# Attention with mixed heads and two dense layers: v fetched later, scores one round later, and a first tile that loads from two queues and writes to three pairs of banks

## Chip, cores and metric

One core of one Trainium2 chip. The metric is the device time of one execution in microseconds (us), median of several runs. Engines are named as in the profile: PE (TensorE matmul), PEld (its weight loads), DVE (VectorE), ACT (ScalarE), POOL (GpSimd), SP (SyncE, which here issues the transfers).

## What is computed

Attention over 4 batches, 12 heads, 448 positions, head size 64, in which the heads are mixed before and after the softmax, and then two dense layers over 448 x 768 a batch. The change touches the attention part alone.

```python
scores = scale * np.matmul(q, k.transpose(0, 1, 3, 2))
scores = np.einsum('bhij,hg->bgij', scores, w_pre)
scores = scores - np.max(scores, axis=-1, keepdims=True)
attn = np.exp(scores)
attn = attn / (np.sum(attn, axis=-1, keepdims=True) + 1e-09)
attn = np.einsum('bhij,hg->bgij', attn, w_post)
return np.matmul(attn, v).astype(np.float32)
```

After it come a gated layer (`_moe_ref`: tanh gelu, a norm, a product over the positions, an output product with the residual) and a second one with sines and cosines (`_moe2_ref`).

## The kernel before

**Tiles and rounds.** Each batch's 448 query rows are cut into tiles of 120, 120, 120 and 88 rows (TILES, line 23): 16 tiles in all, numbered 0 to 15 through the batches; `first` and `last` give a tile's first and last round. A round handles two groups of ten query rows with all their 12 heads. A tile of 120 rows has six rounds, one of 88 rows has five, the last of which holds a single group of eight rows: 92 rounds. Tiles 4, 8 and 12 are the first of batches 1 to 3.

**What a round does** (the loop `for r in range(-LR, NR + 7)`, lines 329 to 358). The order on every engine is the order in which the program issues, written out by hand. Round r issues: `relayout(r + 4)`, two transfers on SP from the tile's score buffer `s` into two of six buffers `blk`; the list `early` (loads and stores); `postmix(r)` on PE; the weights of r + 1 on DVE and POOL (`recip2`, `weigh`); `at_copy(r)` on ACT and DVE; the lists `front` and `mid`; `premix(r + 2)` on PE, `rowmax` on DVE, `expo` on ACT, `recip` on POOL; then the lists `work` and `late`. Each list is filled with `put(list, round, function, arguments)`.

**Scores.** `scores(b, t, c)` makes two of a tile's 12 heads; six units c = 0 to 5 make the tile's `s`. A unit's matmuls (line 130) write two PSUM banks, and ACT copies both with one instruction into `s` (line 137). The pool psA holds one pair of banks; in the first two tiles every other unit takes two banks of psC instead, and DVE copies them (line 134). There are two `s` buffers: tile T's first copy overwrites the buffer of tile T - 2 and waits until that tile's last relayout has landed. `units(T)` (line 277) spreads a tile's six units over the rounds from `first[T - 1] - 4` to `first[T] - 5`. The first unit of a round goes to `front`, ahead of premix; if a round has a second one, it goes to `work`, behind premix. So far a round holds one unit, save the first round of tiles 4, 8 and 12, whose units have five rounds.

**Loads.** All transfers are issued by SP in program order: q of a tile three rounds ahead of its units, k of a batch in the rounds of the units of the tile before the batch's first, v in four parts from round f - 14 on, three rounds apart, f being the batch's first round (line 294); for batch 0 in rounds 1 to 4. v has two buffers, which the batches take in turn. It is read by `attn_v` (lines 242 and 246), whose first unit for a tile stands one round behind the tile's last round. `relayout` (line 148) also waits until the `blk` that it overwrites has been read by `premix` three rounds before.

**The start.** Eight matmuls on zeros warm PE up; SP issues q of tile 0, the six k and small constants; then the six units of tile 0 run, and the loop begins at round -4.

**Beside the rounds** ACT, DVE and POOL decode the weights `w_in` of the first dense layer (lines 484 to 511), in rounds 8 to 85. The dense part follows from about 346 us.

Of the kernel before, what the change touches and what calls it, by code (L numbers as in the profile page):

```python
# [6 lines left out]
F32 = mybir.dt.float32  # L7
# [4 lines left out]
AF = mybir.ActivationFunctionType  # L12
# [4 lines left out]
B, H, S, D = 4, 12, 448, 64  # L17
# [5 lines left out]
TILES = [(t0, min(TI, S - t0)) for t0 in range(0, S, TI)]  # L23
HALF = [n // IB * SQ for t0, n in TILES]
SKIP = [64 - h for h in HALF]
QCOLS = [p + NP * n for p, (t0, n) in zip(SKIP, TILES)]
AW = [-(-n // IB) * SQ for t0, n in TILES]
AM, AX3 = 2 * 3 * H, 2 * 3 * H + H
LR, LQ = 4, 2
# [5 lines left out]
def attention(tc, nc, io, xT, B, extra, tail):  # L35
# [9 lines left out]
    tiles = [(b, t) for b in range(B) for t in range(len(TILES))]  # L45
    nt = len(tiles)
    first, last = {}, {}
# [4 lines left out]
    with ExitStack() as es:  # L52
        early_es = ExitStack()

        def pool(name, bufs, **kw):
            return es.enter_context(tc.tile_pool(name=name, bufs=bufs, reuse_waits="tile", **kw))

        def pool_r(name, bufs, **kw):
            return early_es.enter_context(tc.tile_pool(name=name, bufs=bufs, side="right", reuse_waits="tile", **kw))
# [6 lines left out]
        psA = pool_r("psA", 1, space=PSUM)  # L66
# [7 lines left out]
        psB = pool("psB", 2, space=PSUM)  # L74
        psC = pool("psC", 2, space=PSUM)
# [4 lines left out]
        ps = psC.tile([128, 512], F32, tag="psC", name="warm_ps")  # L80
# [3 lines left out]
        kpre = cp.tile([128, 2, 64], F32, name="kpre")  # L84
# [6 lines left out]

        kt, qt = {}, {}

        def load_k(b, c):
            kt[b, c] = k_p.tile([128, S], F32, tag="k", name="k")
            nc.sync.dma_start(out=kt[b, c], in_=io["kvT"][b, 128 * c:128 * c + 128, 0])

        def load_q(b, t):
            n, o = QCOLS[t], sum(QCOLS[:t])
            qt[b, t] = q_p.tile([128, max(QCOLS)], F32, tag="q", name="q")  # L100
            nc.sync.dma_start(out=qt[b, t][:, :n], in_=io["qT"][b, :, o:o + n])

        vt = [p.tile([128, 4, NP, 128], F32, tag="v", name="v") for p in (vr_p, v_p)]

# [6 lines left out]
        st = {}  # L111

        def scores(b, t, c):

            n = TILES[t][1]
            if c == 0:
                st[b, t] = s_p.tile([128, H, S], F32, tag="s", name="s")
            q, k, o = qt[b, t], kt[b, c], c * n
            m = 64 + n - HALF[t]
            apart = b == 0 and t < 2 and c % 2  # L120
            if apart:
                ps = [psC.tile([128, 512], F32, tag="psC", name="psA") for _ in range(2)]
            else:
                pair = psA.tile([128, 2, 512], F32, tag="psA", name="psA")
                ps = [pair[:, e] for e in range(2)]
            for h in range(2):
                r = slice(64 * h, (64, m)[h])
                for e in range(2):
                    p = slice(64 * e, 64 * e + 64)
                    nc.tensor.matmul(ps[e][r, :S], q[p, o + r.start:o + r.stop], k[p], start=True, stop=True)  # L130
            out = st[b, t][:m, 2 * c:2 * c + 2]
            if apart:
                for e in range(2):
                    nc.vector.tensor_scalar(out=out[:, e], in0=ps[e][:m, :S], scalar1=0.125, scalar2=None,  # L134
                                            op0=ALU.mult)
            else:
                nc.scalar.activation(out=out, in_=pair[:m, :, :S], func=AF.Copy, scale=0.125)  # L137
# [4 lines left out]
        def relayout(r):  # L142
            b, t, k, step, m, n = pairs[r]
            sblk[r] = [blks[2 * (r % 3) + e] for e in range(m)]
            p = 64 - n // 2 * H
            for e, blk in enumerate(sblk[r]):
                o = SKIP[t] + k + e
                nc.sync.dma_start(out=blk[p:p + n * H], in_=st[b, t][o:o + step * (n - 1) + 1:step])

        def premix(r):  # L150
            ps = mix[r] = [psB.tile([128, 512], F32, tag="psB", name="psB") for _ in sblk[r]]
# [120 lines left out]
        early, front, mid, work, late = {}, {}, {}, {}, {}  # L272

        def put(d, r, fn, *a):
            d.setdefault(r, []).append((fn, a))

        def units(T):
            lo, hi = first[tiles[T - 1]] - LR, first[tiles[T]] - LR - 1
            return [lo + (c * (hi - lo + 1)) // NP for c in range(NP)]

        for T in range(1, nt):
            b, t = tiles[T]
            u = units(T)
            for c in range(NP):
                put(front if u[c] not in u[:c] else work, u[c], scores, b, t, c)
            if T > 1:
                put(early, u[0] - QO, load_q, b, t)
            if t == 0:
                for c, r in enumerate(units(T - 1)):
                    put(early, r, load_k, b, c)  # L290
        for b in range(B):
            f = first[b, 0]
            for j in range(4):
                put(early, f - 14 + 3 * j if b else 1 + j, load_v, b, j)
        for T in range(nt):
            b, t = tiles[T]
            for c in range(NP):
                if T == nt - 1:
                    r = last[b, t] + 1 + c // 3
                else:  # L300
                    r = last[b, t] + (min(2 + c, 6) if T == 0 else min(1 + c, 5 if t == 2 else 6))
# [5 lines left out]
        for j, fn in enumerate(extra):  # L307
            r = JR0 + (NR - JR0 - JR1) * j // len(extra)
# [8 lines left out]
            put(early, r + 4, fn[5], dec)  # L317


        load_q(0, 0)  # L320
        for c in range(NP):
            load_k(0, c)
            if c == 1:
                nc.sync.dma_start(out=kpre, in_=io["kpre"].rearrange("p (o c) -> p o c", o=2))
        load_q(0, 1)
        for c in range(NP):
            scores(0, 0, c)
# [785 lines left out]
def build(tc, nc, io, out):  # L1113
    with tc.manual_schedule(), ExitStack() as top:
        dram = top.enter_context(tc.tile_pool(name="scratch", bufs=1, space=bass.MemoryType.DRAM))
        xT = dram.tile([DM, B * S], F32, name="xT")
        x2T = dram.tile([DM, B * S], F32, name="x2T")
        d = Dense(tc, nc, io, xT, x2T, out)
        d.scratch(dram)
        right, left1, left2 = ExitStack(), ExitStack(), ExitStack()  # L1120
        tail, win_es, last_u, end = moe1(d, left1, right)
        th_es = moe2(d, left2, win_es, last_u, left1)
        for i in range(4):
            tail.setdefault(-2 + 2 * i, []).append(d.step)
        slots = top.enter_context(ExitStack())
        d.open_slots(slots)
        jobs = []
        for half, ks in ((1, range(KD)), (0, range(KE))):
            for k in ks:
                jobs += d.decode_tiles(io["w_in"], slice(128 * k, 128 * k + 128), HF * half, HF * half + HF,  # L1130
                                       lambda k=k, half=half: d.pieces(k, half))
        attention(tc, nc, io, xT, B, jobs, tail)
        while d.at < len(d.units):
            d.step()
        th_es.close()
        right.close()
        slots.close()
        left2.close()
# [69 lines left out]
```

## Time and profile before

| | us |
|---|---|
| median of 3 runs | 867.61 (865.63 to 867.61) |
| the profiled execution | 866.24 |
| its span in the trace | 864.5 |
| PE busy | 842.7 (97%) |
| DVE busy | 592.1 (68%) |
| ACT busy | 493.6 (57%) |
| POOL busy | 204.6 (24%) |

The page gives a share of busy time for the whole span, and a chain of work that ended last, followed back from the last instruction. The busy time of PE is that of matmuls that overlap, so a busy PE is not one at its peak. What a round costs is read from the timeline: the distances from the start of a block of matmuls to the start of the next. In timelines, equal neighbours are merged into one line with their count; a bracket at the end tells how long the engine stood idle before, and what ended that.

### The profile page before, as it was taken

How to read it: one execution, taken by the hardware profiler on the slowest of the kernel's cores; microseconds unless marked ns; L12 is line 12 of the kernel's file. 1: busy time of each engine (PE TensorE's matmuls, PEld its weight loads, DVE VectorE, ACT ScalarE, POOL GpSimd, SP SyncE). 2: the span in 40 equal slices, each digit the busy share in tenths (PEclk: the TensorE clock that was granted, in tenths of full speed). 3: DMA queues.
4: the chain of work that ended last, by engine and by line, in shares of the span. 5: the costliest groups of instructions: out<-in, count | busy, mean ns of one | idle time of the engine just before them, and what ended most of it. 6: DMA issues, size and time to landing. Idle time of an engine off the chain costs nothing.

```text
span 864.5 us, 27167 instructions
## 1 busy us (share of the span) xinstructions
PE 842.7 (97%) x10984; PEld 664.9 (77%) x10984; DVE 592.1 (68%) x1364; ACT 493.6 (57%) x1106; POOL 204.6 (24%) x404
## 2 busy tenths in 40 slices
PE   7999999899989999999999999999999999999998
PEld 2465666466656666798988989898999999999997
DVE  5566676467666776879999998779784378338231
ACT  3688788579877886584845767247443155025010
POOL 0222223122222222000000000038228047306321
PEclk9999999899999999999999999999999999999999
DMA  5667657565776546551757867997611221300301
GB/s 195 212 223 227 196 180 229 179 201 172 249 202 209 177 158 167 153 159 50 247 180 240 270 196 230 351 299 230 214 38 45 83 54 31 118 19 1 118 11 64
DMA packets 108877, 142.16 MB, mean 164 GB/s; under 512 B 25680, under 2 KB 94800, under 8 KB 108752
## 3 DMA queue, kind: packets, MB, share of 16 engines
q1 hardware_dynamic: 108752, 140.42, 51.4%
q8 instruction: 87, 1.43, 0.7%
q14 instruction: 38, 0.31, 0.1%
HBM read 74.26 MB, written 27.59 MB: 118 GB/s over the span
## 4 chain that ended last, share of the span: by engine, by line
PE 91%; issue 3%; DMA 2%; DVE 2%; ACT 1%; POOL 0%; ACTq 0%; POOLq 0%; DVEq 0%; SPq 0%
PE ps L442 55%; PE psB L156 8%; PE psD L242 8%; PE psA L130 8%; PE psC L201 7%; PE psD L246 3%; DMA blk<-s 2%; PE psC L206 1%; PE ps L960 1%; DMA x<-x2T 1%; ACT s L137 0%; ACT e L170 0%; DVE s L134 0%; POOL x2s L438 0%; POOL z L438 0%
## 5 line engine op out<-in xcount | busy, mean ns | idle before, releaser
L170 ACT ACTIVATE e<-psB,nmx 128x448 f32<-128x448 f32 x180 | 112.3, 629 | 49.0 <-DVE nmx L162 47.3
L162 DVE TENSOR_REDUCE nmx<-psB 128x1 f32<-128x448 f32 x180 | 104.1, 619 | 27.9 <-PE psB L156 26.1
L442 PE MATMUL ps<-wtok,z 128*128 128x448 f32 x504 | 104.8, 368 | 0.0
L130 PE MATMUL psA<-k,q 64*64 64x448 f32 (+2 forms) x768 | 93.7, 547 | 10.1 <-ACT s L137 8.0
L242 PEld LDWEIGHTS psD<-at,v 128*64 128x64 f32 x1152 | 56.5, 137 | 60.6 <-issue 39.9
L442 PEld LDWEIGHTS ps<-wtok,z 128*128 128x128 f32 x504 | 94.6, 188 | 9.5
L156 PE MATMUL psB<-blk,kpre 64*64 64x448 f32 x720 | 97.9, 541 | 1.9 <-DMA blk<-s 1.1
L442 PE MATMUL ps<-wth,x2s 128*128 128x384 f32 x504 | 94.2, 342 | 2.4 <-POOL x2s L438 1.8
L137 ACT ACTIVATE s<-psA 124x896 f32<-124x896 f32 (+1 forms) x90 | 82.7, 919 | 24.0 <-PE psA L130 12.2
L438 POOL TENSOR_TENSOR x2s<-x,x2s 128x384 fp32r<-128x384 f32 x28 | 28.8, 1047 | 278.2 <-DMA xres<-xT 201.8
L442 PEld LDWEIGHTS ps<-wth,x2s 128*128 128x128 f32 x504 | 88.1, 188 | 4.1 <-POOL x2s L438 2.8
L442 PE MATMUL ps<-u,wch 128*128 128x448 f32 x432 | 89.9, 368 | 0.0
L442 PEld LDWEIGHTS ps<-u,wch 128*128 128x128 f32 x432 | 81.0, 188 | 8.1
L201 PE MATMUL psC<-wr,e 64*64 64x60 f32 x4320 | 83.4, 220 | 1.7 <-issue 1.1
L201 PEld LDWEIGHTS psC<-wr,e 64*64 64x64 f32 x4320 | 74.1, 136 | 8.6 <-POOL wr L188 5.3
L242 PE MATMUL psD<-at,v 128*64 128x120 f32 (+1 forms) x1152 | 77.3, 269 | 0.0
L438 POOL TENSOR_TENSOR z<-zz,z 128x384 fp32r<-128x384 f32 x56 | 63.8, 1159 | 56.4 <-ACT z L435 56.3
L435 ACT ACTIVATE u<-xres 128x448 fp32r<-128x448 f32 x24 | 13.8, 577 | 98.1 <-DVE xres L1021 98.1
L156 PEld LDWEIGHTS psB<-blk,kpre 64*64 64x64 f32 x720 | 36.7, 132 | 42.5 <-issue 19.3
L176 POOL TENSOR_SCALAR rc<-sum 128x2 f32<-128x2 f32 (+1 forms) x92 | 17.9, 195 | 210.5 <-ACT e L170 210.5
L188 POOL TENSOR_SCALAR wr<-wts,rc 128x60 f32<-128x60 f32 x180 | 54.1, 314 | 48.1 <-DVE rc L181 36.5
L442 PE MATMUL ps<-slot,x 128*128 128x512 f32 x252 | 60.1, 396 | 0.0
(111 smaller groups left out, 1437.6 us busy)
## 6 DMA issues: line engine op xcount, KB each, us to landing
blk<-s SPq DMA_DIRECT2D x176, 210.0 KB
draw<-in_w_in SPq DMA_DIRECT2D x24, 256.0 KB
k<-in_kvT SPq DMA_DIRECT2D x24, 224.0 KB
xraw<-xT SPq DMA_DIRECT2D x24, 224.0 KB
xres<-xT SPq DMA_DIRECT2D x24, 224.0 KB
x2T<-xres SPq DMA_DIRECT2D x24, 224.0 KB
xres<-x2T SPq DMA_DIRECT2D x24, 224.0 KB
out<-uu SPq DMA_DIRECT2D x24, 224.0 KB
```

The source lines that it names most:

```text
L130: nc.tensor.matmul(ps[e][r, :S], q[p, o + r.start:o + r.stop], k[p], start=True, stop=True)
L137: nc.scalar.activation(out=out, in_=pair[:m, :, :S], func=AF.Copy, scale=0.125)
L156: nc.tensor.matmul(ps[e][c:c + 64, :S], kpre[k, e], blk[k], start=True, stop=True)
L162: nc.vector.tensor_reduce(out=nmx[r][:, e:e + 1], in_=ps[:, :S], axis=AX.X, op=ALU.max, negate=True)
L170: nc.scalar.activation(out=x, in_=ps[:, :S], func=AF.Exp, bias=m[:, e:e + 1], accum_out=sm[:, e:e + 1])
L176: nc.gpsimd.tensor_scalar(out=rc[:, :m], in0=sm[:, :m], scalar1=1e-9, scalar2=1.0, op0=ALU.add, op1=ALU.mult)
L188: nc.gpsimd.tensor_scalar(out=w, in0=wts, scalar1=rc[:, e:e + 1], scalar2=0.0, op0=ALU.mult, op1=ALU.add)
L201: nc.tensor.matmul(pc[r][h][c:c + 64, o:o + H], x[p, 128 * jc + c:128 * jc + c + 64], w[p], start=(e == 0 and jc == 0), stop=(not two and ...
L242: nc.tensor.matmul(ps[p], v[:, jc, p], main[:, H * jc + 2 * c + i], start=(o == 0 and jc == 0), stop=False)
L246: nc.tensor.matmul(px[p] if e else ps[p, 0], v[q, 3, p], rest[q, 2 * c + i], start=(o == 0 and e == 1), stop=(o > TI))
L438: eng.tensor_tensor(out=out, in0=in_, in1=hi.bitcast(F32), op=ALU.subtract)
L442: self.nc.tensor.matmul(ps, l, r, start=(i == 0), stop=(i == len(terms) - 1))
```

## The change

1. `load_v` for batches 1 to 3 goes from rounds f - 14, - 11, - 8, - 5 to f - 3, - 1, + 1, + 3.
2. `units(T)` begins one round later for every tile but tile 1, and ends in the same round. `load_q`, which stands three rounds ahead of the first unit, and the k loads, which use `units`, move with it.
3. In tile 0 the units take psA, psC and psB in turn (c % 3). Of a unit in psB, ACT copies one bank and DVE the other.
4. At the start, q of tile 0 is loaded in two parts, the first with what units 0 and 1 need; k 0, 2, 4 and kpre are issued by ACT, k 1, 3, 5 by SP.
5. In rounds 0 to 2 the second of a relayout's two transfers is issued by ACT.

```diff
--- before.py
+++ after.py
@@ -91,14 +91,15 @@
 
         kt, qt = {}, {}
 
-        def load_k(b, c):
+        def load_k(b, c, eng=nc.sync):
             kt[b, c] = k_p.tile([128, S], F32, tag="k", name="k")
-            nc.sync.dma_start(out=kt[b, c], in_=io["kvT"][b, 128 * c:128 * c + 128, 0])
-
-        def load_q(b, t):
-            n, o = QCOLS[t], sum(QCOLS[:t])
+            eng.dma_start(out=kt[b, c], in_=io["kvT"][b, 128 * c:128 * c + 128, 0])
+
+        def load_q(b, t, parts=None):
+            o = sum(QCOLS[:t])
             qt[b, t] = q_p.tile([128, max(QCOLS)], F32, tag="q", name="q")
-            nc.sync.dma_start(out=qt[b, t][:, :n], in_=io["qT"][b, :, o:o + n])
+            for m, n in parts or ((0, QCOLS[t]),):
+                nc.sync.dma_start(out=qt[b, t][:, m:n], in_=io["qT"][b, :, o + m:o + n])
 
         vt = [p.tile([128, 4, NP, 128], F32, tag="v", name="v") for p in (vr_p, v_p)]
 
@@ -117,9 +118,10 @@
                 st[b, t] = s_p.tile([128, H, S], F32, tag="s", name="s")
             q, k, o = qt[b, t], kt[b, c], c * n
             m = 64 + n - HALF[t]
-            apart = b == 0 and t < 2 and c % 2
+            apart = b == 0 and (c % 3 if t == 0 else t == 1 and c % 2)
             if apart:
-                ps = [psC.tile([128, 512], F32, tag="psC", name="psA") for _ in range(2)]
+                p, tag = (psC, "psC") if apart == 1 else (psB, "psB")
+                ps = [p.tile([128, 512], F32, tag=tag, name="psA") for _ in range(2)]
             else:
                 pair = psA.tile([128, 2, 512], F32, tag="psA", name="psA")
                 ps = [pair[:, e] for e in range(2)]
@@ -131,6 +133,9 @@
             out = st[b, t][:m, 2 * c:2 * c + 2]
             if apart:
                 for e in range(2):
+                    if apart == 2 and not e:
+                        nc.scalar.activation(out=out[:, e], in_=ps[e][:m, :S], func=AF.Copy, scale=0.125)
+                        continue
                     nc.vector.tensor_scalar(out=out[:, e], in0=ps[e][:m, :S], scalar1=0.125, scalar2=None,
                                             op0=ALU.mult)
             else:
@@ -145,7 +150,8 @@
             p = 64 - n // 2 * H
             for e, blk in enumerate(sblk[r]):
                 o = SKIP[t] + k + e
-                nc.sync.dma_start(out=blk[p:p + n * H], in_=st[b, t][o:o + step * (n - 1) + 1:step])
+                eng = nc.scalar if e and r < 3 else nc.sync
+                eng.dma_start(out=blk[p:p + n * H], in_=st[b, t][o:o + step * (n - 1) + 1:step])
 
         def premix(r):
             ps = mix[r] = [psB.tile([128, 512], F32, tag="psB", name="psB") for _ in sblk[r]]
@@ -275,7 +281,7 @@
             d.setdefault(r, []).append((fn, a))
 
         def units(T):
-            lo, hi = first[tiles[T - 1]] - LR, first[tiles[T]] - LR - 1
+            lo, hi = first[tiles[T - 1]] - LR + (T > 1), first[tiles[T]] - LR - 1
             return [lo + (c * (hi - lo + 1)) // NP for c in range(NP)]
 
         for T in range(1, nt):
@@ -291,7 +297,7 @@
         for b in range(B):
             f = first[b, 0]
             for j in range(4):
-                put(early, f - 14 + 3 * j if b else 1 + j, load_v, b, j)
+                put(early, f - 3 + 2 * j if b else 1 + j, load_v, b, j)
         for T in range(nt):
             b, t = tiles[T]
             for c in range(NP):
@@ -317,11 +323,12 @@
             put(early, r + 4, fn[5], dec)
 
 
-        load_q(0, 0)
+        n = 2 * TILES[0][1] + SKIP[0]
+        load_q(0, 0, ((0, n), (n, QCOLS[0])))
         for c in range(NP):
-            load_k(0, c)
-            if c == 1:
-                nc.sync.dma_start(out=kpre, in_=io["kpre"].rearrange("p (o c) -> p o c", o=2))
+            load_k(0, c, (nc.scalar, nc.sync)[c % 2])
+            if c == 0:
+                nc.scalar.dma_start(out=kpre, in_=io["kpre"].rearrange("p (o c) -> p o c", o=2))
         load_q(0, 1)
         for c in range(NP):
             scores(0, 0, c)
```

## Rows read from the trace of the kernel before

**Rows 1.** The page's chain of work that ended last, shares of the span.
```profile
PE 91%; issue 3%; DMA 2%; DVE 2%; ACT 1%; POOL 0%; ACTq 0%; POOLq 0%; DVEq 0%; SPq 0%
```

**Rows 2.** Timeline of PE, ordinary round: start us, us, engine, line, count, [idle].
```profile
58.52 0.84 PE L242 MATMUL psD<-at,v 128*64 128x120 f32 x12
...
59.45 0.88 PE L201 MATMUL psC<-wr,e 64*64 64x60 f32 x48
...
60.27 0.93 PE L130 MATMUL psA<-k,q 64*64 64x448 f32 x8
61.02 0.93 PE L156 MATMUL psB<-blk,kpre 64*64 64x448 f32 x8
61.88 0.84 PE L242 MATMUL psD<-at,v 128*64 128x120 f32 x12
```

**Rows 3.** Timeline of PE, two rounds of the last tile without scores.
```profile
320.60 1.49 PE L156 MATMUL psB<-blk,kpre 64*64 64x448 f32 x8
...
323.76 1.47 PE L156 MATMUL psB<-blk,kpre 64*64 64x448 f32 x8
```

**Rows 4.** Timeline of PE, rounds beside the weighted sum of an 88-row tile.
```profile
287.55 0.93 PE L156 MATMUL psB<-blk,kpre 64*64 64x448 f32 x8
288.41 0.69 PE L242 MATMUL psD<-at,v 128*64 128x90 f32 x12
...
290.76 0.93 PE L156 MATMUL psB<-blk,kpre 64*64 64x448 f32 x8
```

**Rows 5.** Timeline of PE, second scores of tiles 4, 8, 12.
```profile
74.97 0.98 PE L130 MATMUL psA<-k,q 64*64 64x448 f32 x8 [1.29 <-ACT s L137]
75.88 0.84 PE L242 MATMUL psD<-at,v 128*64 128x120 f32 x12
...
78.39 0.93 PE L156 MATMUL psB<-blk,kpre 64*64 64x448 f32 x8
...
159.01 1.76 PE L130 MATMUL psA<-k,q 64*64 64x448 f32 x8 [4.25 <-ACT s L137]
...
164.97 0.54 PE L156 MATMUL psB<-blk,kpre 64*64 64x448 f32 x4
...
243.35 0.98 PE L130 MATMUL psA<-k,q 64*64 64x448 f32 x8 [2.17 <-ACT s L137]
```

**Rows 6.** Timelines of SP (issues) and of ACT ahead of tile 8's first copy.
```profile
147.53 0.63 SPq L108 DMA_DIRECT2D v<-in_vN  x1
148.26 1.05 SPq L476 DMA_DIRECT2D draw<-in_w_in  x1
149.41 1.69 SPq L148 DMA_DIRECT2D blk<-s  x2
...
158.04 0.92 ACT L137 ACTIVATE s<-psA 124x896 f32<-124x896 f32 x1 [4.11 <-DMA blk<-s]
```

**Rows 7.** Busy time by stretch; last: granted PE clock, DMA share, GB/s.
```profile
160.00:162.00 2.00, 2.00 (x20) 1.09 (x12) 0.00 (x0) 1.75 (x5) 0.19 (x1) 0.50 0.85 247
```

**Rows 8.** Timeline of ACT in the ordinary round: copy of scores, second exponential.
```profile
61.27 0.92 ACT L137 ACTIVATE s<-psA 112x896 f32<-112x896 f32 x1
...
63.37 0.62 ACT L170 ACTIVATE e<-psB,nmx 128x448 f32<-128x448 f32 x1
63.89 0.20 ACT L170 ACTIVATION_READ_ACCUMULATOR e<-psB,nmx 128x1 f32 x1
```

**Rows 9.** Timeline of all engines, from warm-up to first premix.
```profile
1.20 3.34 PE L82 MATMUL warm_ps<-warm 128*128 128x512 f16 x8 [1.20 <-DVE warm L79]
...
10.95 1.15 DVE L134 TENSOR_SCALAR s<-psA 124x448 f32<-124x448 f32 x2 [1.07 <-PE psA L130]
...
12.18 6.84 SPq L148 DMA_DIRECT2D blk<-s  x8
...
15.11 1.50 PE L156 MATMUL psB<-blk,kpre 64*64 64x448 f32 x5 [1.14 <-DMA blk<-s]
16.01 0.14 PEld L156 LDWEIGHTS psB<-blk,kpre 64*64 64x64 f32 x3 [0.71 <-DMA blk<-s]
```

**Rows 10.** Busy time by stretch at the start, columns as in group 7.
```profile
2.00:8.00 6.00, 5.32 (x35) 1.85 (x37) 2.97 (x7) 0.95 (x3) 0.00 (x0) 1.00 0.97 338
13.50:20.00 6.50, 4.64 (x32) 1.07 (x24) 2.64 (x7) 2.26 (x5) 0.59 (x3) 1.00 0.63 239
```

## Prediction, written before the changed kernel was built or run

> **What bounds the kernel now.** I read the chain that ended last first [rows 1]: 91% of the span is TensorE, and only small pieces are something else ("DMA blk<-s" 2%, "issue" 3%). So a change gains only where TensorE stands still, and it loses wherever it makes TensorE stand still. The change touches the attention part (to about 346 us of 864.5); what follows is TensorE from end to end and moves with it.
>
> Next the timeline of TensorE in an ordinary round [rows 2]. I call the blocks V (weighted sum, line 242 and 246), M (postmix, 201 and 206), S (scores, 130) and P (premix, 156). They stand back to back: V 0.93 us from start to start (58.52 to 59.45), M 0.82, S 0.75, P 0.86: a round is 3.36 us, and TensorE sets it. In the last tile's rounds, which hold no S, a round is 3.16 us (320.60 to 323.76) although TensorE has only 2.6 us of work: there P is drawn out to 1.48 us, because the loop premix, row maximum, exponential, premix (two banks) sets the pace [rows 3]. A round without S is thus only 3.36 - 3.16 = 0.20 us shorter. That number carries the forecast. While V runs on an 88-row tile's 90 columns the round is 3.21 us [rows 4].
>
> Last, where TensorE stands still. Three rounds (tiles 4, 8 and 12, the first tile of batches 1 to 3) hold two S units. There ACT's copy of the first unit waits for the relayout transfers of the tile two back, whose buffer it overwrites, and TensorE waits for the copy, since the one pair of banks psA is busy: 1.29, 4.25 and 2.17 us [rows 5]. The second shows the cause best: the last relayout was issued from 149.41 on, not two microseconds behind a part of v, and ACT stood 4.11 us until 158.04 [rows 6].
>
> **Part 1: scores one round later.** units() starts a tile's six units one round later and ends them in the same round. Six units that had six rounds now have five: the first round holds none, the second holds two. For tiles 4, 8 and 12 (five rounds) it becomes four rounds, two of them double, where there was one.
>
> What it removes: the waits. Of each gap, 0.29 us would be there in any double round (P's row ends 0.93 after its start, at 61.95; the second S could start at 62.24, below). 1.29 + 4.25 + 2.17 - 3 x 0.29 = 6.84 us. After the 4.25 us, TensorE ran at 0.50 of its clock, that is at 1.2 instead of 2.4 GHz [rows 7]: from the late S to the next P took 5.96 us (159.01 to 164.97), where tile 4 took 3.42 (74.97 to 78.39), 2.54 us more [rows 5]. Together 9.4 us. One round more is 3.2 us and part 2 lightens the queue, so I take all of it away.
>
> What it adds: the price of a unit that is second in its round. In the ordinary round, ACT copies the first unit from 61.27 to 62.19 [rows 8] and TensorE follows 0.05 us later (74.92 to 74.97 in [rows 5]), at 62.24; without a second unit V would have started at 61.88 [rows 2]. That is 0.36 us of waiting. The unit itself takes 0.91 us (74.97 to 75.88). Then the next round's S needs psA again: its copy stands on ACT behind both exponentials, whose last reading ends at 63.89 + 0.20 = 64.09 [rows 8], so it ends at 65.01 and S may start at 65.06; TensorE would be there at 61.88 + 0.36 + 0.91 + 0.93 + 0.82 = 64.90. Another 0.15 us. A second unit costs 1.42 us, the empty round gives back 0.20: 1.22 us for a tile. Where V is short (tiles 6, 10, 14) the empty round gives back 3.21 - 3.16 = 0.05 and the wait for psA is 0.15 longer: 1.42 + 0.15 - 0.05 = 1.52 us. Tiles 2 to 15 are affected; 4, 8 and 12 get one more double and one empty round, the same 1.22. Tile 2 has no V beside its units; I give it 1.22 too, with 0.6 and 2.3 as ends. Sum: 11 x 1.22 + 3 x 1.52 = 18.0 us. The three doubles that exist today will have the 0.15 us wait again once ACT is no longer late, 0.45, so the stalls give back 8.9 net.
>
> From below, a second unit would cost only its matmuls less the empty round (0.75 - 0.20 = 0.55 a tile, 7.7 us in all) if ACT's copies were hidden; from above 1.6 a tile plus 2.3 (some 23 us), where w_in's decoding puts two more ACT instructions ahead of the second copy.
>
> **Part 2: v ten rounds later.** The same twenty transfers. v is first read six rounds after its batch's first tile begins, and the last quarter is issued three rounds after that begin: three rounds, 10 us, cover a landing that at the worst place today took about 7.6 us (150.3 to 158.0 in [rows 6]). The new place has no k loads beside it. I cost it at nothing; what is queued behind v on SP is the next relayout, needed two rounds later. Uncovered, each late v would cost what it is late. Its gain is already in part 1's 9.4.
>
> **Part 3: the first tile.** Today TensorE's six units alternate between psA and psC and end with DVE's copies at 10.95 + 1.15 = 12.10; the relayouts go out from 12.18, all on SP, eight in 6.84 us (0.855 each), and premix begins at 15.11 and its second half of blocks at 16.01 [rows 9]. With three pairs of banks TensorE can run its units 0.85 us apart from the end of the warm-up at 4.54 and is done at 9.7; the last half copies end near 10.4 by DVE's 0.58 a half. That is 1.7 us. The second block goes out on ACT at the same time as the first on SP, so it doesn't land 0.9 us later, but perhaps 0.3 later since both share the engines: 0.6 us. Together 2.3 us; ends 0.5 (k lands no earlier than it does) and 3.2. ACT now carries three relayout issues of 0.855 us ahead of its copies of tile 1's units; who waits for those is TensorE's third unit of tile 1, and that is hidden behind the relayout's landing (premix near 13.7).
>
> Here a row and a rule speak to each other. While k is loaded (2 to 8 us) the core moves 338 GB/s, while only relayouts run (13.5 to 20 us) 239 GB/s [rows 10]: I read the relayouts as paced by their issue, and two issuers as a help. The Trainium skill, "DMA: Bandwidth & Descriptors", section "Issuing engines are not separate DMA queues", says that transfers from several engines run on the same 16 DMA engines and that a second issuer saves only the issue time, usually small beside the transfer. By it, two blocks of 215 KB at 338 GB/s would take 1.27 us instead of 1.71, and the first tile would give 2.1 instead of 2.3 us, an estimate; the row agrees that k is limited by the transfer, not that relayouts are.
>
> **The sum.** +18.0 - 8.9 - 2.3 = +6.8 us. The profiled execution took 866.24 us (span 864.5), 1.4 under the median of the three runs shown (867.61): 873.0 by the one, 874.4 by the other. I say 874.0.
>
> **The rivals.**
> 1. The second unit is nearly free and the change is faster. If TensorE loses only 0.55 us a tile, +7.7 - 8.9 - 2.3 = -3.5, about 863.5. The point from which it decides is (8.9 + 2.3) / 14 = 0.8 us a tile. For it: a round has slack in the loop of [rows 3]. Against: the copy of 0.92 us starts only when S is done and P covers 0.86 less the pipe, and tile 4's row shows the 0.91 us.
> 2. In between: the waits cost about 0.8 to 0.9 a tile, or the first tile gives 3 us and more: 865 to 869, no change.
> 3. v meets other loads in its new place, and relayouts land late there: TensorE waits as at tile 8 in one or two of the batches, with the clock's fall. Each such place costs 4 to 6 us: 878 to 884. Against: no k is fetched there.
> 4. One round more doesn't do what it says: the 7.6 us of landing remain, and tile 8 still waits. A wait of 7.6 - 2 x 3.2 = 1 us at one tile: 875, within the forecast.
>
> **How the numbers follow.** Forecast with rival 4: 0.60 (869.5 to 878). Rival 1: 0.15. Rival 2: 0.17. Rival 3: 0.08. A measurement of this kernel tells 0.3%, 2.6 us, from no change. Faster 0.15, within 0.17, slower 0.68. The range 864 to 879 leaves out most of rival 3 and the lower half of rival 1.
>
> **What would show it.** In the changed kernel's timeline of TensorE, tile by tile, a round with no S and P near 1.4 us, then a round in which V starts 1.3 us later than usual after P, S standing between with an idle time put down to "ACT s". If those waits are missing or the rounds stay at 3.36 on average, part 1's price is wrong. The waits of ACT's copies for "DMA blk<-s" (8.9 us now) should be near nothing; if not, rival 4. The first premix should begin near 13.7 us instead of 15.11, with its second half right behind. Relayout waits of TensorE in the rounds around a batch's begin would be rival 3.

## The result, and the profile after

The changed kernel takes 871.51 us (median of 6 executions, 870.39 to 874.83); the kernel before, beside it, 867.61 (865.63 to 870.59). The ratio is 1.0057, with a 95% interval of 1.0030 to 1.0084: slower by 4.9 us, 2.6 to 7.3. In a later comparison (run "changed_again" below) it is 1.0070, 1.0046 to 1.0094. Forecast were 874.0 us and +6.8. The execution that was profiled took 874.33 us, with a span of 872.5.

From the changed kernel's page, the shares of the span in the chain that ended last (compare [rows 1]):

```profile
PE 82%; DVE 6%; DMA 5%; ACT 4%; issue 2%; SPq 1%; POOL 0%; DVEq 0%; ACTq 0%; POOLq 0%
```

TensorE still sets most of the time. What follows the attention takes as long as before: 518.17 us before and 518.31 after from its first matmul to the end. The whole difference lies in the attention.

TensorE's timeline in tile 3 of the changed kernel (start us, us, engine, line, operands, count, idle time ahead and what ended it). The lines have moved: 248 is V, 207 M, 132 S, 162 P; 142 is ACT's copy of the scores.

```profile
51.96 0.84 PE L248 MATMUL psD<-at,v 128*64 128x120 f32 x12
53.70 1.54 PE L162 MATMUL psB<-blk,kpre 64*64 64x448 f32 x8
55.18 0.84 PE L248 MATMUL psD<-at,v 128*64 128x120 f32 x12
...
58.89 0.97 PE L132 MATMUL psA<-k,q 64*64 64x448 f32 x8 [0.29 <-ACT s L142]
59.79 0.84 PE L248 MATMUL psD<-at,v 128*64 128x120 f32 x12
...
63.25 0.84 PE L248 MATMUL psD<-at,v 128*64 128x120 f32 x12
```

Start of V to start of V: the round without S takes 55.18 - 51.96 = 3.22 us, its P drawn out to 1.54; the round with two S takes 59.79 - 55.18 = 4.61, with an idle 0.29 us ahead of the second S, put down to ACT's copy; the next takes 63.25 - 59.79 = 3.46. Together 11.29 us where three ordinary rounds of 3.36 [rows 2] take 10.08: 1.21 us more. The prediction had 1.22.

The same in tile 6, where V has 90 columns:

```profile
116.05 0.69 PE L248 MATMUL psD<-at,v 128*64 128x90 f32 x12
119.21 0.69 PE L248 MATMUL psD<-at,v 128*64 128x90 f32 x12
123.69 0.69 PE L248 MATMUL psD<-at,v 128*64 128x90 f32 x12
125.74 0.98 PE L132 MATMUL psA<-k,q 64*64 64x448 f32 x8 [0.27 <-ACT s L142]
127.40 0.69 PE L248 MATMUL psD<-at,v 128*64 128x90 f32 x12
```

127.40 - 116.05 = 11.35 us. Three rounds of 3.21 [rows 4] would be 9.63, but one of these three is 3.43 us in the kernel before as well: there they take 9.85, from the postmix at 111.43 to the one at 121.28. So the price is 1.5 us, as in tiles 10 and 14; the prediction had 1.52. The S of the round behind the double one waits too, 0.27 us. In tile 2 four rounds take 14.60 us from postmix to postmix (30.98 to 45.58), where they took 13.04 (28.34 to 41.38): 1.56 us more.

What TensorE waited for ahead of S, from the changed kernel's view of waits (us in total, times, longest), and what ACT's copies waited for, from the view of line 142 (us in total, times):

```profile
PE psA L132 <- ACT s L142: 8.2, 20, 2.0
  DMA blk<-s: 0.3, 2
```

ACT's waits for the relayouts, 8.9 us in five copies before ([rows 6] has the longest), are down to 0.3 in two. TensorE's wait for psA was 8.0 us in 4 places before; now it is 8.2 us in 20: a few long waits have become many short ones. Most are the price of the second units; 1.99 us are at the start, below.

So at a batch's begin the change does what the prediction said, at its price. At the start of the kernel it doesn't. In one list, the changed kernel's start (ACTq and SPq are the issues of ACT and SP; 154 is the relayout, 139 DVE's half copies):

```profile
4.72 1.77 PE L132 MATMUL psA<-k,q 64*64 64x448 f32 x8
7.06 7.23 PE L132 MATMUL psA<-k,q 64*64 64x448 f32 x56 [0.57 <-DMA k<-in_kvT]
13.86 11.17 SPq L154 DMA_DIRECT2D blk<-s  x7
13.86 1.40 ACTq L154 DMA_DIRECT2D blk<-s  x1
15.31 0.92 ACT L142 ACTIVATE s<-psA 124x896 f32<-124x896 f32 x1 [1.91 <-DVE s L139]
16.28 0.98 PE L132 MATMUL psA<-k,q 64*64 64x448 f32 x8 [1.99 <-ACT s L142]
17.75 1.89 PE L162 MATMUL psB<-blk,kpre 64*64 64x448 f32 x8 [0.49 <-DMA blk<-s]
```

Busy time by stretch there: the stretch, its length, busy PE, PEld, DVE, ACT and POOL (instructions), the granted clock of TensorE, DMA share, GB/s:

```profile
18.00:20.00 2.00, 2.00 (x12) 0.95 (x15) 0.33 (x1) 0.24 (x1) 0.00 (x0) 0.50 0.64 209
```

The relayouts go out at 13.86 us, later than the 12.18 of before [rows 9] and not near 10.4; premix begins at 17.75 instead of 15.11; TensorE stands 1.99 us for ACT's copy; and right behind that its clock falls to 0.50, 1.2 instead of 2.4 GHz. Part of this belongs to this one execution, as the runs show.

### The profile page after: what moved, and what is told of

Read it like the earlier page. It is cut to its first block, busy times and chain, and to the rows that moved or that the text cites. A ratio compares the mean times of both kernels' runs of the same rounds, so it can differ in the third digit from the quotient of the medians.

```text
span 872.5 us, 27116 instructions
## 1 busy us (share of the span) xinstructions
PE 851.7 (98%) x10984; PEld 662.3 (76%) x10984; DVE 591.2 (68%) x1364; ACT 494.0 (57%) x1107; POOL 205.1 (24%) x404
## 4 chain that ended last, share of the span: by engine, by line
PE 82%; DVE 6%; DMA 5%; ACT 4%; issue 2%; SPq 1%; POOL 0%; DVEq 0%; ACTq 0%; POOLq 0%
PE ps L449 48%; PE psB L162 8%; PE psA L132 8%; PE psD L248 7%; PE psC L207 6%; PE psD L252 3%; DMA blk<-s 2%; ACT s L142 2%; DMA xres<-xT 1%; PE psC L212 1%; ACT e L176 1%; DMA wch<-wch_d 1%; DMA x2T<-xres 1%; DMA k<-in_kvT 1%; PE ps L967 1%
## 5 line engine op out<-in xcount | busy, mean ns | idle before, releaser
L162 PE MATMUL psB<-blk,kpre 64*64 64x448 f32 x720 | 103.4, 548 | 1.7 <-ACT at L224 0.7
L132 PE MATMUL psA<-k,q 64*64 64x448 f32 (+2 forms) x768 | 94.5, 565 | 10.3 <-ACT s L142 8.2
L142 ACT ACTIVATE s<-psA 124x896 f32<-124x896 f32 (+1 forms) x89 | 81.6, 917 | 15.7 <-PE psA L132 10.6
L207 PE MATMUL psC<-wr,e 64*64 64x60 f32 x4320 | 81.0, 219 | 0.5
L182 POOL TENSOR_SCALAR rc<-sum 128x2 f32<-128x2 f32 (+1 forms) x92 | 17.9, 194 | 216.1 <-ACT e L176 194.8
L162 PEld LDWEIGHTS psB<-blk,kpre 64*64 64x64 f32 x720 | 34.4, 133 | 42.9 <-issue 21.3
```

The source lines that it names most:

```text
L162: nc.tensor.matmul(ps[e][c:c + 64, :S], kpre[k, e], blk[k], start=True, stop=True)
L182: nc.gpsimd.tensor_scalar(out=rc[:, :m], in0=sm[:, :m], scalar1=1e-9, scalar2=1.0, op0=ALU.add, op1=ALU.mult)
L207: nc.tensor.matmul(pc[r][h][c:c + 64, o:o + H], x[p, 128 * jc + c:128 * jc + c + 64], w[p], start=(e == 0 and jc == 0), stop=(not two and ...
```

## The experiments

The theory: a double round costs 1.2 us because psA is one pair of banks; the change pays that fourteen times, takes away the late copies, and gains nothing from v beyond that. The rivals: v is what takes the late copies away and the scores only cost; or the first tile is what makes the difference. All results, each a ratio to the kernel before on the same chip:

| run | what it holds | median us (executions) | ratio, 95% interval |
|---|---|---|---|
| scores_later | part 1 alone | 874.93 (4) | 1.0114, 1.0077 to 1.0151 |
| v_later | part 2 alone | 861.16 (10) | 0.9937, 0.9907 to 0.9967 |
| first_tile | part 3 alone | 867.54 (10) | 1.0007, 0.9978 to 1.0036 |
| no_scores_later | parts 2 and 3 | 860.75 (10) | 0.9926, 0.9897 to 0.9954 |
| without_v_later | parts 1 and 3 | 873.7 (5) | 1.0091, 1.0064 to 1.0119 |
| changed_again | all three | 872.22 (7) | 1.0070, 1.0046 to 1.0094 |
| split_copy | all three, copy split | 876.48 (4) | 1.0108, 1.0045 to 1.0171 |
| double_second_round | before, double moved | 864.17 (10) | 0.9961, 0.9932 to 0.9991 |
| both_v_and_double | parts 2, 3, double moved | 858.74 (4) | 0.9895, 0.9842 to 0.9949 |
| relayouts_by_sp | part 3 without ACT's relayouts | 868.24 (10) | 1.0020, 0.9987 to 1.0053 |
| v_double_old_start | part 2, double moved | 859.26 (6) | 0.9918, 0.9889 to 0.9948 |
| v_double_banks | the same, three pairs of banks | 859.7 (6) | 0.9915, 0.9884 to 0.9945 |

**scores_later**, part 1 alone, on the kernel before:

```diff
-            lo, hi = first[tiles[T - 1]] - LR, first[tiles[T]] - LR - 1
+            lo, hi = first[tiles[T - 1]] - LR + (T > 1), first[tiles[T]] - LR - 1
```

> Only the scores' rounds move (before + one round later). Theory (each tile pays about 1.2 us for an empty round and a second unit, 14 tiles): 14 to 18 us added, less the waits of tiles 4, 8, 12. If one round is enough for the relayouts with v where it was, the waits fall by 8 to 9 us and the kernel is 6 to 9 us slower than before; if v's transfers still hold them up, 10 to 15 us slower. Rival (TensorE loses only the matmuls, 0.55 us a tile): within 2 us of before.

Measured: +1.14%, 9.9 us (6.7 to 13.1), where 6 to 9 were expected; part 1's sum in the prediction is 18.0 - 8.9 = 9.1. ACT's waits for the relayouts are gone by this part alone (this run's view of the copies' line):

```profile
  DMA blk<-s: 0.3, 2
```

So v isn't needed to remove them once the scores come later, and the scores cost more than the removal gives.

**v_later**, part 2 alone, on the kernel before:

```diff
-                put(early, f - 14 + 3 * j if b else 1 + j, load_v, b, j)
+                put(early, f - 3 + 2 * j if b else 1 + j, load_v, b, j)
```

> Only v is fetched later. Theory (v, k, q and w_in loads together made the relayouts late at tiles 4, 8, 12): the waits of 1.3, 4.3 and 2.2 us and the fall of the clock after the second go, 6 to 9 us faster than before. Rival (k, q and w_in alone make them late, v only stands beside): under 2 us faster, and ACT's copies of tiles 4, 8 and 12 still wait for blk<-s by 1 us and more.

Measured: -0.63%, 5.5 us less (2.9 to 8.1), where 6 to 9 were expected. The waits of ACT's copies in all, the two copies that wait, SP's issues ahead of the second and behind its begin, and the stretch behind it (columns as above):

```profile
  DMA blk<-s: 5.7, 2
155.34 0.92 ACT L137 ACTIVATE s<-psA 124x896 f32<-124x896 f32 x1 [1.42 <-DMA blk<-s]
177.72 0.92 ACT L137 ACTIVATE s<-psA 124x896 f32<-124x896 f32 x1 [4.33 <-DMA blk<-s]
166.98 1.31 SPq L476 DMA_DIRECT2D draw<-in_w_in  x1
168.40 5.89 SPq L148 DMA_DIRECT2D blk<-s  x3
177.04 0.50 SPq L108 DMA_DIRECT2D v<-in_vN  x1
178.00:182.00 4.00, 3.46 (x21) 0.88 (x17) 1.70 (x6) 4.00 (x10) 0.79 (x3) 0.57 0.58 168
```

Tile 8's wait falls from 4.11 [rows 6] to 1.42 us, and those of tiles 4 and 12 are gone. Tile 9's, 1.23 us before, is 4.33 here, with the clock's fall behind it. That looks like rival 3 of the prediction and isn't: the relayout that this copy waits for, the last one of tile 7, is the first of the three issued from 168.40 on, behind a part of w_in, and from 138 us on no part of v was issued until 177.04, when ACT had stood for 3.65 us. What made it late stays open.

TensorE's waits for psA are 3.6 us in all, where they were 8.0. But the profiled execution was the slowest of the ten (867.78 us), with 5.3 us of the idle time that the last section is about, so the 5.5 us can't be added up from it. The executions of the comparison bear the gain out: TensorE's mean granted clock was 0.990 to 0.999 in the 25 of the kernel before, never 1.000, and 1.000 in seven of the ten of v_later.

**first_tile**, part 3 alone: the changed kernel with the two lines above put back.

> Only the first tile is changed. In the changed kernel's trace the first 37 us took 2.6 us longer than before, with TensorE at half clock up to 10.6 us and again from 17.4 to 20.9. Theory 1 (that clock was the draw of one execution): this kernel's median is 1.5 to 3 us faster than before, its runs spread by 3 us or more according to the clock, and a profile with full clock from about 4 us has premix at 13.5 to 14.5. Theory 2 (the change itself costs: a k part lands late and TensorE stands): 1 to 3 us slower in the median, and the late k shows in the profile whatever the clock.

Measured: +0.07%, with an interval of 0.3% to both sides. The 2.3 us of the prediction are not there, and neither theory came true. This run's start, in one list:

```profile
11.40 6.66 SPq L154 DMA_DIRECT2D blk<-s  x5
11.40 1.40 ACTq L154 DMA_DIRECT2D blk<-s  x1
12.85 0.92 ACT L142 ACTIVATE s<-psA 124x896 f32<-124x896 f32 x1 [1.92 <-DVE s L139]
13.82 0.98 PE L132 MATMUL psA<-k,q 64*64 64x448 f32 x8 [2.00 <-ACT s L142]
15.28 1.10 PE L162 MATMUL psB<-blk,kpre 64*64 64x448 f32 x8 [0.48 <-DMA blk<-s]
```

The relayouts go out 0.78 us earlier than before, but premix is no earlier (15.28; 15.11 and 16.01 before [rows 9]). From the issue, both blocks need 3.88 us, as the second did before (16.01 - 12.18 = 3.83): a second issuer brings the second block no earlier. ACT, whose queue holds the issue, waits for DVE's last half copy, then issues for 1.40 us; only then does it copy tile 1's first unit, and TensorE's third unit stands 2.00 us for it.

**no_scores_later**, parts 2 and 3: the changed kernel with part 1 undone.

```diff
-            lo, hi = first[tiles[T - 1]] - LR + (T > 1), first[tiles[T]] - LR - 1
+            lo, hi = first[tiles[T - 1]] - LR, first[tiles[T]] - LR - 1
```

> The changed kernel with the scores back in their old rounds (v later and first tile stay). Theory: it saves the price of 14 empty rounds and second units, about 14 us against the changed kernel, and v later alone keeps the waits small: 8 to 10 us faster than the kernel before, 857 to 860 us. Rival (the scores' extra round is what removes the waits): waits of 1 to 4 us at tiles 4, 8, 12 come back and it is within 3 us of before.

Measured: -0.74%, 6.4 us less than before (4.0 to 8.9), not to be told apart from v_later. It is less than the 8 to 10 expected, and the rival's sign is there in part: ACT's copies wait for relayouts again, 4.9 us in four, and TensorE stands 1.47 us for the copy in tile 8 and 1.68 in tile 12. Still it is part 1 that turns a gain into a loss: between this (-6.4) and the changed kernel (+4.9) lie 11.3 us, where part 1 alone cost 9.9. Beside the later v, about half of the waits that part 1 removes are gone already.

**split_copy** asks whether the 0.29 us wait for psA enters the time. In the changed kernel, the copy of a first unit that has a second behind it is divided between ACT and DVE:

```diff
+            elif split:
+                nc.scalar.activation(out=out[:, 0], in_=pair[:m, 0, :S], func=AF.Copy, scale=0.125)
+                nc.vector.tensor_scalar(out=out[:, 1], in0=pair[:m, 1, :S], scalar1=0.125, scalar2=None,
+                                        op0=ALU.mult)
```

> The changed kernel, but where a round holds two units, ACT copies one bank of the first and DVE the other, so that psA is free 0.35 us earlier. Nothing else moves. Theory (of the price of a second unit 0.36 us is waiting for that copy, 17 such units): TensorE's idle of 0.29 us ahead of each second unit goes, 4 to 6 us faster than the changed kernel, some 866 to 868 us. Rival (the price is the matmuls alone, the wait is covered anyway): under 1.5 us faster.

Measured: 876.48 us, 5.0 more than the changed kernel's median, 3.3 to 4.4 more by the two ratios that it has to the kernel before: the opposite of what I had expected. Tile 4's double round in this run, all engines, and the wait in its view of waits (line 143 is DVE's half here):

```profile
78.11 0.58 DVE L228 COPY at<-psC 128x420 f32<-128x420 f32 x1
78.27 0.55 ACT L142 ACTIVATE s<-psA 124x448 f32<-124x448 f32 x1
78.85 0.62 DVE L143 TENSOR_SCALAR s<-psA 124x448 f32<-124x448 f32 x1 [0.16 <-ACT s L142]
79.53 0.98 PE L132 MATMUL psA<-k,q 64*64 64x448 f32 x8 [0.58 <-DVE s L143]
PE psA L132 <- DVE s L143: 10.4, 17, 1.0
```

DVE's half doesn't run beside ACT's but behind it, from 78.85 on, also behind DVE's own copy of at. So psA comes free later and TensorE stands 0.58 us instead of 0.29. The miss is an answer all the same: from postmix to postmix this round takes 4.92 us (76.45 to 81.37), where it takes 4.63 in the changed kernel (78.44 to 83.07). The wait is 0.29 us longer and so is the round, here and in 12 of the other 16 double rounds; the last four grow by more. A longer wait for psA enters the time in full, as part 1's sum took it to. The edit didn't make the wait shorter, so what its absence would give wasn't measured.

**double_second_round**: the kernel before, with the double of tiles 4, 8 and 12 in the second round instead of the first, so that it stays one double for a tile and comes one round later:

```diff
-            return [lo + (c * (hi - lo + 1)) // NP for c in range(NP)]
+            return [lo + (c * (hi - lo + 1) + 1) // NP for c in range(NP)]
```

> The kernel before, but for tiles 4, 8 and 12 the second unit stands in the second of the five rounds instead of the first (no empty round, as many doubles as before, v where it was). TensorE no longer needs psA right behind the copy that waits for the relayout. Theory (ACT works in order, so its wait is handed on to the exponentials and one round later to TensorE): tile 4's wait of 1.1 us is hidden, of the longer ones 1 to 1.7 us each; 3 to 6 us faster than before, more if the clock doesn't fall. Rival 1 (the wait is hidden as a whole): 8 to 9 us faster. Rival 2 (nothing is hidden): within 1.5 us.

Measured: -0.39%, 3.4 us less; 3 to 6 were expected. It isn't a whole cure, as tile 4 shows (timelines of ACT and TensorE in this run):

```profile
  DMA blk<-s: 4.7, 3
75.61 0.92 ACT L137 ACTIVATE s<-psA 124x896 f32<-124x896 f32 x1 [2.91 <-DMA blk<-s]
76.58 0.98 PE L130 MATMUL psA<-k,q 64*64 64x448 f32 x8 [1.27 <-ACT s L137]
```

**both_v_and_double**: parts 2 and 3 with that same line in units().

> v later and the first tile as changed, scores in their old rounds, the second unit of tiles 4, 8 and 12 in their second round. With v later ACT waits 1.2 to 1.9 us there, short enough to be hidden for the most part: 2 to 4 us faster than the same kernel without the last step (860.8 us), so 857 to 859 us. If short waits are handed on to the exponentials too, no difference to 860.8.

Measured: 858.74 us, 0.9895 (0.9842 to 0.9949): some 9 us less than before, the lowest median of all, and within the 857 to 859 expected. v_double_old_start, below, can't be told apart from it. Its waits for relayouts:

```profile
  DMA blk<-s: 0.4, 1
```

They are as good as gone, as with part 1, without the fourteen doubles.

**relayouts_by_sp**: first_tile, with all relayouts on SP again.

```diff
-                eng = nc.scalar if e and r < 3 else nc.sync
+                eng = nc.sync
```

> The first tile alone, but SP issues all relayouts. In the kernel with the first tile alone the two blocks of round 0 went out together at 11.40 from SP and ACT, landed 0.9 us apart, and ACT, held by its issue, copied tile 1's first unit late, so that TensorE stood 2.0 us. Theory (two issuers move the blocks no faster): the second block lands as early, ACT's copy comes 1 us earlier or more, TensorE's idle of 2 us is gone; total 0 to 1.5 us faster than with ACT's issues. Rival (the second issuer saves its 0.8 us a block): premix begins 0.6 us later and the total is as much slower.

Measured: +0.20%, -0.13 to +0.53: no difference that this measurement can tell, neither to before nor to first_tile, where 0 to 1.5 us less were expected. Its start, TensorE's timeline and SP's issue:

```profile
13.83 7.36 SPq L154 DMA_DIRECT2D blk<-s  x8
14.55 0.98 PE L132 MATMUL psA<-k,q 64*64 64x448 f32 x8 [0.30 <-ACT s L142]
16.73 2.03 PE L162 MATMUL psB<-blk,kpre 64*64 64x448 f32 x5 [1.21 <-DMA blk<-s]
17.72 0.22 PEld L162 LDWEIGHTS psB<-blk,kpre 64*64 64x64 f32 x3 [0.80 <-issue]
```

TensorE's 2.00 us are 0.30 now, so they were ACT's issue. But the blocks are there 2.90 and 3.89 us after the issue, no later than with two issuers, and TensorE waits for them instead. What ACT's issue cost was nearly hidden, and what it was to bring wasn't there.

**changed_again**: the changed kernel once more.

> The changed kernel once more, in more rounds and beside the next three, to settle how far it is from the kernel before: 3.9 us by the medians, 4.9 by the ratio, 8.1 by the two profiled executions. Theory (price of second units about 15, waits 9, first tile 0 to 1, a fetch of instructions now and then on both sides): 4 to 7 us slower. Rival (parts help each other and it is nearer): under 3 us.

Measured: 1.0070, that is +6.0 us (4.0 to 8.1); the prediction's sum was +6.8. Again the clock fell at the start (columns as above):

```profile
16.00:19.00 3.00, 3.00 (x19) 1.04 (x15) 1.16 (x2) 1.34 (x4) 0.07 (x1) 0.51 0.65 200
```

**without_v_later**: the changed kernel with v's line put back, so parts 1 and 3.

```diff
-                put(early, f - 3 + 2 * j if b else 1 + j, load_v, b, j)
+                put(early, f - 14 + 3 * j if b else 1 + j, load_v, b, j)
```

> The changed kernel with v in its old rounds. Theory (one round more already takes the relayout waits away, so v has nothing left to give): within 1.5 us of the changed kernel, and no copy of scores waits for blk<-s. Rival (v's old place costs something besides those waits, as the 3.8 us between the kernel with later scores alone and the changed kernel suggest): 3 us slower than the changed kernel or more.

Measured: 873.7 us, 1.5 more than the changed kernel in the same comparison, with intervals that overlap (1.0064 to 1.0119 and 1.0046 to 1.0094). ACT's waits for relayouts are 0.3 us in 2, as with v later. Whether v later brings one or two microseconds beside part 1 isn't settled by this; no wait for relayouts says that it does, and this profile has 2.8 us of the idle time of the last section, where changed_again's has 0.3.

**v_double_old_start** and **v_double_banks**: the kernel before with v's line and the line of double_second_round, the second with three pairs of banks for the first tile as well (none of the other loads or issues of part 3):

```diff
-            apart = b == 0 and t < 2 and c % 2
+            apart = b == 0 and (c % 3 if t == 0 else t == 1 and c % 2)
```

> v later and the second unit of tiles 4, 8, 12 in their second round, start as before. Theory (the first tile as changed gives 0 to 1 us in the middle of its runs): 6 to 8 us faster than before, 858 to 861 us, and within 1.5 us of the same with the first tile as changed (858.7).

> The one before, and three pairs of banks in the first tile; loads and relayouts all by SP in their old order. Theory (the banks end the first tile's scores 1 to 1.7 us earlier; the second issuer only delays k and holds ACT): relayouts go out at 10.5 to 11.3 where the clock rose near 4 us, TensorE's idle of 2 us ahead of the first premix isn't there, 1 to 2 us faster than v_double_old_start. Rival (the loads, not the banks, set the first tile): no difference.

Measured: 0.9918 and 0.9915, with intervals of 0.3% to both sides. Two changed lines give what both_v_and_double gives with part 3, within what can be told apart. The third pair of banks was to give 1 to 2 us and adds nothing that can be measured, though the relayouts go out at 11.68 us and TensorE doesn't stand 2 us there.

## Why the prediction was right, and where not

**Part 1's price** held: +18.0 us was the sum, and tile by tile the trace has 1.21 in tile 3 (predicted 1.22), 1.5 in the three tiles with a short V (1.52) and 1.56 in tile 2 (1.22, ends 0.6 and 2.3). Of its terms, the empty round's gift (0.20) shows in P's 1.54 us and a round of 3.22 instead of 3.16, the wait for the copy was put at 0.36 by the starts and shows as 0.29 of idle time on TensorE, and the 0.15 us of the next S shows as a round of 3.46 instead of 3.36. split_copy shows that a longer wait enters the time in full. Rival 1, a nearly free second unit, needed less than 0.8 us a tile. (The copy's end at 74.92 is not in [rows 5]; it is ACT's 74.00 + 0.92.)

**The stalls**, -8.9, held: ACT's waits, which happen to add up to the same 8.9 us, are down to 0.3, so rival 4 is out, and the clock doesn't fall at tile 8. scores_later alone came to +9.9 where 18.0 - 8.9 gives 9.1. But the 8.9 was read from one execution. With the same loads and scores around tiles 4, 8 and 12, TensorE stood for the copy 1.29, 4.25 and 2.17 us before, 1.29, 0.32 and 0.98 in first_tile, and 1.42, 2.62 and 0.28 in relayouts_by_sp.

**Part 2** at nothing held inside the change, to within some 2 us that weren't settled, and rival 3 didn't come about. The reason, that its gain is already in part 1's, was right only for this combination: alone, it gives 5.5 us, and it is a cheaper cure than part 1. I had worked out no price for the parts apart.

**Part 3**, -2.3 us, is the term that failed: by the runs it is +0.6, -1.9 to +3.1. Three steps of it were off.

1. "The last half copies end near 10.4." The relayouts go out at 11.0 to 11.2 where the start ran well (without_v_later, split_copy, both_v_and_double), not at 10.4. I spaced the units 0.85 us from 4.54 on and left out that the second unit waits for its k: in both_v_and_double, the units stand at 4.58 and, after a wait for k of 0.61, at 6.16, and the last one is ready for its copies at 10.20. Before, the second k was there at once (16 matmuls in one piece of 1.73 us from 4.71). The rest is DVE, which copies three halves in a row, from 9.45 to 11.14. The late k was the low end that the prediction named (k lands no earlier than it does).
2. "The second block lands perhaps 0.3 later" than the first, for 0.6 us. Both blocks are there 3.9 us after the first issue with one issuer and with two (3.83, 3.88, 3.89). I read the relayouts as paced by their issue [rows 10]; they aren't. The Trainium skill, "DMA: Bandwidth & Descriptors", section "Issuing engines are not separate DMA queues", had the right side: a second issuer saves only the time of issuing. Even the 2.1 us by that rule was too much, since the estimate let the two blocks move at the rate of k.
3. "That is hidden behind the relayout's landing", of ACT's issues. Nearly so: from the relayouts' issue to the first postmix it is 8.0 us in the five profiles with the old start and 8.16 in first_tile. But where TensorE's clock fell behind its idle time, 8.5 to 9.0 (the changed kernel 22.82 - 13.86 = 8.96). It fell in five of the seven profiles with ACT's issues, in one of the two with the new banks and SP's issues alone, and in none of the five with the old start. I had not asked what an idle TensorE does to its clock there, though [rows 7] show it at tile 8.

With the same pace of the start, the first postmix begins at 20.14 to 20.27 with the old start (before, v_later, v_double_old_start) and at 19.95 to 20.19 with the new one (without_v_later, split_copy, both_v_and_double): 0.1 us for 2.3. Where the clock didn't fall (first_tile, no_scores_later, v_double_banks) it begins at 19.57 to 19.78.

**What the sum left out.** By the terms that held the sum is 18.0 - 8.9 + 0 = +9.1 us, above the measured +4.9 and +6.0. The traces show where the rest is. From the first postmix to the last (by the packed traces), the kernel before takes 323.4 us and the changed one 328.7 and 328.2 in its two profiles, 5.3 and 4.8 more. I compared each round with the shortest that it takes in any profile of its kind: nine with the old scores, four with part 1 (split_copy left out). Between these shortest rounds the fourteen tiles cost 17.9 us more with part 1. Above them, the kernel before loses 9.3 us in the rounds of tiles 4, 8 and 12, which are the stalls, and another 4.9 us in single rounds of other tiles; the changed kernel loses nothing in the former and 1.6 and 0.9 us in the latter. So 3 to 4 us of gain come from rounds that the prediction took as undisturbed. One of them is in tile 9 of the kernel before, 4.32 us from postmix to postmix instead of 3.36:

```profile
180.19 0.87 PE L201 MATMUL psC<-wr,e 64*64 64x60 f32 x46
181.71 0.26 PE L201 MATMUL psC<-wr,e 64*64 64x60 f32 x1 [0.64 <-issue]
184.51 0.70 PE L201 MATMUL psC<-wr,e 64*64 64x60 f32 x36
```

All nine profiles with the old scores lose 4.0 to 11.7 us in this way, the four with part 1 only 0.9 to 3.7. Why they are fewer with part 1 wasn't tested. That the forecast came within 1 or 2 us is thus partly luck: part 3's 2.3 us and these 3 to 4 go opposite ways. The two large terms, the price and the stalls, were not luck. without_v_later (+7.9, 5.5 to 10.3), whose profile loses 3.7 us in such rounds, is nearer the 9.1.

## What to carry to other kernels

Where TensorE sets the pace and the rounds are full, don't empty one round to fill the next twice: the empty one gives back only the slack of its other loops (0.2 us here), while the double pays for its work and for the turn of its single pair of banks, a price that can be read off the trace of before. If a buffer comes free too late, first look at what is queued ahead of its last reader: moving that load, one line, gave 5.5 us here, where moving the work cost 9.9. And an engine that issues a transfer is held by what that transfer waits for and by the issue itself (1.40 us here), with no faster landing in return.

## What the runs showed of the hardware that I had not expected

**The start's pace.** The same warm-up runs in all fourteen profiles, yet TensorE's first units run at full pace from some 3.9 us on in one and from 10.6 in another. TensorE's timeline in both_v_and_double, whose start is the changed kernel's:

```profile
4.58 0.98 PE L132 MATMUL psA<-k,q 64*64 64x448 f32 x8
6.16 5.49 PE L132 MATMUL psA<-k,q 64*64 64x448 f32 x56 [0.61 <-DMA k<-in_kvT]
```

In the changed kernel's profile, above, the first unit took 1.77 us and the next 56 matmuls 7.23. That moves the relayouts' issue (11.22 and 13.86), and it accounts for 2.6 us of the 8.1 between the two profiled executions, where the medians differ by 4 to 6. It goes with the execution and not with the change: scores_later, which has the old start, issued them at 13.38 instead of 12.18. That it is TensorE's clock is argued from two things. The durations are those at 0.50 elsewhere (1.76 us for eight such matmuls in [rows 5]). And the first record of the granted clock, at full, stands at 10.62 us in the changed kernel's packed trace and at 4.36 in both_v_and_double's, from 3.87 to 10.62 in the fourteen; the view reads 1.00 before it too, for want of a record. What decides it stays open.

**Idle time that ends with "issue".** Some of TensorE's idle time ends with "issue", with no semaphore behind it. The list of DMA queues names a candidate, a queue q8 of the kind "instruction". From first_tile's page (packets, MB, share), from its DMA view for 66.4 to 67.6 us and from TensorE's timeline:

```profile
q8 instruction: 87, 1.43, 0.7%
q8 instruction: 1, 0.02, 5.2%
68.99 0.27 PE L207 MATMUL psC<-wr,e 64*64 64x60 f32 x3 [2.24 <-issue]
```

That one packet, 16 KB, has landed at 67.55 us by the packed trace, and the idle time ends 1.44 us later. It is so every time: between 18 and 350 us the fourteen profiles have 54 idle times of this kind on TensorE, and each ends 1.27 to 1.71 us after a packet of q8 has landed, although these packets come only every 3.4 to 8.7 us (first_tile and before). That points to TensorE waiting for its next instructions. No run changed that, and what makes a packet late stays open.

The sum of these idle times is 7.8 us here, 5.3 in v_later, 0.2 in the changed kernel, 1.3 before. That is as much as the parts that are compared, so one profiled execution against another can't settle a difference of a few microseconds; the ratios over several executions can.
